# A fused attention and MLP kernel on one core: single-chunk blocks in the opening, w_in rounded at another place, two separating products in place of eight, and other places for the attention visits of groups 1 and 2

## The chip, the cores and the metric

The kernel runs on one core of a Trainium2 chip. The metric is device microseconds of one execution. The kernel before took 205.94 us (median of three runs, 205.86 to 206.51).

The engines carry short names: PE multiplies matrices (PEld is its weight load, which lies beside the multiplication), DVE is the vector engine, ACT the scalar engine with its activation tables, POOL the GpSimd engine, SP the engine that issues plain transfers. Each works through its own queue of instructions in order and waits on semaphores for the others.

## The reference

Linear attention with a decay for each head runs over 4 batches, 8 heads, 768 positions and 64 columns. Its output, put together over heads, is the input of an MLP with an exact GELU.

```
for b in range(nb):                                  # blocks of 64 positions
    intra = (qb @ kb.T * Dmask) @ vb                 # Dmask[i, j] = lam ** (i - j) for i >= j, else 0
    inter = (qb * lam_pow) @ kv_state                # lam_pow = lam ** (pos + 1)
    out   = intra + inter
    kv_state = lam ** block * kv_state + (kb * rev_pow).T @ vb     # rev_pow = lam ** (block - 1 - pos)
x = out.transpose(0, 2, 1, 3).reshape(3072, 512)
h = x @ w_in                                         # 512 x 2048
g = 0.5 * h * (1 + erf(h / sqrt(2)))
return g @ w_out                                     # 2048 x 512
```

## The kernel before

**Tiling.** The kernel takes blocks of 128 positions, which it calls chunks. There are 24: chunk n belongs to position block n // 4 and batch n % 4. Four chunks, one of each batch, make a group of 512 tokens; there are six groups. A chunk needs q, k and v (loaded by POOL with a conversion to bf16, line 68), k and q transposed (`kT`, `qT`), the scores k q in PSUM, masked by DVE into `sc_m` (line 201), and an output product from `sc_m` and the values (line 235). From its second position block on it also needs the product of q with the carried state (line 228). The output, emptied from PSUM into `x_t` (`empty_outputs`, lines 243 to 251), is the MLP's input, already transposed.

**MLP of a group.** The first product (`mm1`, line 421) takes 16 column tiles of `w_in`, called kf, each over four slices of the contraction, into a PSUM bank with the tag `mh`, and ACT applies the GELU (line 424) into `g_t`. A block of it can take several kf and only some of the tokens. In group 0 the second product is plain (`mm2`, line 434: 16 blocks, first those of chunks 0 and 1 in turn, then those of chunks 2 and 3). In groups 1 to 5 it is made of seven half-size products (`blocks_by_seven`, line 317) that run in the order m3, m4, m5, m2, m1, m6, m7, each for u = 0 and 1. Their left sides are sums of quarters of `g_t`, made on DVE (`g_sum`, line 291, each in two halves), and sums of the results on DVE follow (lines 355 to 401). The bank of m1 is read by DVE (line 387) before m7 adds to it again.

**PSUM.** A tag has two buffers in turn for `sc`, `mh` and `mo`, and one for `o` and `t`. A new tile in a buffer waits until the last reader of the old one is done.

**Order of the work.** The schedule is written by hand. Before the first MLP block the opening runs chunks 0 and 1 and the transposes of chunk 2, with idle products (`keep_warm`, line 484) between. In group 0 the dictionary `group0` (line 556) says which attention steps stand ahead of which block. For the rest, `at(when, run)` sorts steps by a place: g plus a share of the group's work, where B is one block of 2048 columns' worth. `visit(done, asked)` (line 588) puts attention products of two chunks at a time between blocks: for the chunks in `done` the state products in two turns and the output products, for those in `asked` the scores. Where there are chunks in `done` but none in `asked`, `apart_ps` (line 602) puts products of zeros between the two turns. `states_of` adds the products for the next state (line 209). `masks`, `empties`, `sums` and `new_states` are the DVE and ACT steps behind a visit.

**Loads.** POOL issues all loads of q, k, v, of `w_in` (but its first 256 columns) and of `w_out`, and between them scales the values (`v_dec`, line 155). The first 256 columns of `w_in` come by SP as float32 (`wide_w`, line 76) and ACT rounds them (line 512). From chunk 8 on, kT and qT are made by transposing transfers that SP issues (lines 176 and 177).

## Time and profile before

| | before |
|---|---|
| median of three runs | 205.94 us |
| the profiled execution, its own time | 206.0 us |
| span of the profiled execution | 204.2 us |
| PE busy | 197.0 us, 96% |
| DVE busy | 124.8 us, 61% |
| POOL busy | 96.2 us, 47% |
| ACT busy | 80.7 us, 39% |
| PE from its first idle product to its first MLP product | 1.19 to 14.29 us |
| group 0: first product, then second product | 14.29 to 32.27, 32.27 to 50.69 us |
| group 1: first product, then the seven products | 50.69 to 67.22, 67.22 to 82.81 us |
| group 2: first product | 82.81 to 100.25 us |

A stage is read as the PE's stretch from the first product of one kind to the first of the next; attention products lie within the stages. The start of an instruction is a point on one clock for all engines. The time of the execution is 1.8 us more than the span.

### The profile page before, as it was taken

The numbers are of one execution on the slowest core, as the hardware profiler recorded it, in microseconds if no ns is written. First come the engines' busy times: TensorE is split into PE (matmuls) and PEld (weight loads), VectorE is DVE, ScalarE is ACT, GpSimd is POOL, SyncE is SP. The second block draws the span as 40 slices with busy tenths as digits, with TensorE's granted clock in tenths as the row PEclk, the third lists the DMA queues.
The fourth block names the chain that finished last, engine by engine and source line by source line (L and its number), as shares of the span: only waits on it lengthen the run. The fifth ranks groups of instructions, "written<-read, shape, count | busy, mean of one in ns | idle before, by whom it ended". The sixth has DMA issues, their size and how long they took to land. (4 is left out here: it accounts for less than half of the span.)

```text
span 204.2 us, 4909 instructions
## 1 busy us (share of the span) xinstructions
PE 197.0 (96%) x2105; PEld 131.2 (64%) x2105; DVE 124.8 (61%) x202; ACT 80.7 (39%) x142; POOL 96.2 (47%) x112
## 2 busy tenths in 40 slices
PE   7889999999999999999999999999999999999992
PEld 2457574556874888646678646688645788445881
DVE  3743426773574699845999815968807857132482
ACT  4946653324565400273520273520264510477200
POOL 8999963899998922599998402000000000000000
PEclk9999999999999999999999999999999999999999
DMA  5999999999999999799999992200500000500014
GB/s 114 156 174 176 199 207 194 155 215 158 178 194 141 154 157 152 232 126 160 117 162 155 231 189 55 56 0 3 206 1 3 0 0 3 205 0 0 3 51 154
DMA packets 102373, 24.70 MB, mean 121 GB/s; under 512 B 92880, under 2 KB 99536, under 8 KB 102352
## 3 DMA queue, kind: packets, MB, share of 16 engines
q0 software_dynamic: 80688, 13.37, 89.4%
q1 hardware_dynamic: 21664, 11.02, 26.8%
q8 instruction: 16, 0.26, 0.5%
q14 instruction: 5, 0.04, 0.1%
HBM read 27.27 MB, written 6.29 MB: 164 GB/s over the span
## 5 line engine op out<-in xcount | busy, mean ns | idle before, releaser
L424 ACT ACTIVATE g_t<-h_ps 128x512 bf16<-128x512 f32 (+2 forms) x101 | 58.2, 576 | 82.0 <-PE h_ps L421 81.8
L421 PE MATMUL h_ps<-x_t,w_in_t 128*128 128x512 bf16 (+3 forms) x488 | 87.0, 334 | 0.4
L421 PEld LDWEIGHTS <-w_in_t 128*128 128x128 bf16 x488 | 44.1, 98 | 38.0 <-issue 1.3
L291 DVE TENSOR_TENSOR g_sum<-g_t 128x1024 bf16<-128x1024 bf16 x50 | 35.6, 752 | 12.6 <-ACT g_t L424 12.6
L317 PEld LDWEIGHTS <-g_sum 128*128 128x128 bf16 x400 | 38.6, 98 | 5.7 <-DVE g_sum L291 0.7
L155 POOL TENSOR_TENSOR v_dec<-v_t,lam_m 128x512 bf16<-128x512 bf16 x23 | 24.8, 1109 | 22.5 <-PE o_ps L235 10.2
L201 DVE TENSOR_TENSOR sc_m<-sc_ps,cmask 128x512 bf16<-128x512 f32 x40 | 25.4, 681 | 13.0 <-PE sc_ps L195 13.0
L68 POOL DMA_DIRECT2D k_t<-in_k_dram x24 | 22.3, 928 | 1.9 <-DMA w_out_t<-in_moe_w_out_dram 1.7
L68 POOL DMA_DIRECT2D v_t<-in_v_dram x24 | 21.7, 906 | 3.0 <-DMA w_out_t<-in_moe_w_out_dram 1.7
L68 POOL DMA_DIRECT2D q_t<-in_q_dram x24 | 21.8, 910 | 2.4 <-DMA w_out_t<-in_moe_w_out_dram 2.2
L317 PE MATMUL r_ps<-w_sum,g_sum 128*128 128x256 bf16 x160 | 19.1, 273 | 0.0
L317 PEld LDWEIGHTS <-g_t 128*128 128x128 bf16 x160 | 15.7, 98 | 2.9
L434 PE MATMUL o_ps<-w_out_t,g_t 128*128 128x512 bf16 x64 | 15.2, 379 | 0.0
L215 DVE TENSOR_TENSOR tmp<-kv_ps,state 128x512 f32<-128x512 f32 x8 | 5.1, 684 | 12.8 <-PE kv_ps L209 12.8
L251 DVE TENSOR_TENSOR x_t<-o_ps,lam_q 128x512 bf16<-128x512 f32 x16 | 10.5, 680 | 1.0 <-PE o_ps L235 1.0
L317 PE MATMUL p_ps<-w_out_t,g_sum 128*128 128x256 bf16 x80 | 9.7, 273 | 0.4 <-DVE g_sum L291 0.4
L434 PEld LDWEIGHTS <-g_t 128*128 128x128 bf16 x64 | 5.9, 98 | 6.2
L484 PE MATMUL idle_ps<-idle 128*128 128x256 bf16 (+1 forms) x33 | 8.6, 400 | 1.2 <-DVE idle L102 1.2
L317 PE MATMUL s_ps<-w_sum,g_sum 128*128 128x256 bf16 x80 | 9.6, 273 | 0.0
L317 PE MATMUL p_ps<-w_sum,g_t 128*128 128x256 bf16 x80 | 9.6, 273 | 0.0
L317 PE MATMUL q_ps<-w_sum,g_t 128*128 128x256 bf16 x80 | 9.6, 273 | 0.0
L317 PE MATMUL q_ps<-w_out_t,g_sum 128*128 128x256 bf16 x80 | 9.6, 273 | 0.0
(68 smaller groups left out, 153.4 us busy)
## 6 DMA issues: line engine op xcount, KB each, us to landing
out_dram<-o_sb SPq DMA_DIRECT2D x9, 512.0 KB, 2.8
k_t<-in_k_dram POOLq DMA_DIRECT2D x24, 128.0 KB, 6.9
q_t<-in_q_dram POOLq DMA_DIRECT2D x24, 128.0 KB, 7.4
v_t<-in_v_dram POOLq DMA_DIRECT2D x24, 128.0 KB, 7.3
w_out_t<-in_moe_w_out_dram POOLq DMA_DIRECT2D x4, 512.0 KB, 10.1
w_in_t<-in_moe_w_in_dram POOLq DMA_DIRECT2D x7, 256.0 KB, 7.3
out_dram<-o_sb SPq DMA_DIRECT2D x5, 256.0 KB, 6.0
wide_w<-in_moe_w_in_dram SPq DMA_DIRECT2D x1, 512.0 KB, 4.1
```

What stands on the lines that cost most here:

```text
L68: nc.gpsimd.dma_start(raw[n, name], chunk_of(name, n))
L155: eng.tensor_mul(c.v_dec, c.v, lam_m[:, :, None].to_broadcast((128, H, D)))
L201: nc.vector.tensor_mul(c.sc_m[:, :, hi, :], c.sc_ps[hi], mask)
L215: nc.vector.tensor_add(tmp, kv_ps, states[n])
L251: nc.vector.tensor_mul(c.x_o, c.o_ps, lam_q)
L291: nc.vector.tensor_tensor(gsum[i][:, ks, :], g_t[:, ka + k:ka + k + n4, ta], g_t[:, kb + k:kb + k + n4, tb], op=op)
L317: nc.tensor.matmul(o, left[i](k, slice(u * C, (u + 1) * C)), right[i](k), start=(begin and k == 0), stop=(k == KH - 1), skip_group_check=True)
L421: nc.tensor.matmul(h_ps[:, k, :], w_in_t[:, ki, (kf + k) * 128:(kf + k + 1) * 128], x_t[:, ki, cols], start=(k == 0 and ki == 0), stop=(ki ...
L424: nc.scalar.activation(g_t[:, kf:kf + ks, cols], h_ps, ACT.Gelu)
L434: nc.tensor.matmul(om[io], g_t[:, kf, io * C:(io + 1) * C], w_out_t[:, kf, :], start=(kf == 0), stop=(kf == NK2 - 1))
L484: nc.tensor.matmul(idle_ps[0][:, :cols], idle[:, :128], idle[:, :cols], start=True, stop=True)
```

## The change

- **Chunk 0's output** is emptied by DVE and no longer by ACT.
- **w_in** is rounded at the head of ACT's constants, before `make_powers`, and no longer behind chunk 0's output.
- **The opening** ends behind the scores of chunk 1. The outputs of chunk 1, the transposes of chunk 2 and idle products become steps of `group0`. The transposes of chunk 3 are split into k ahead of one block and q ahead of the next; k's use the bank `t`, and its scores follow at once.
- **Group 0's plan** for the first product has 19 blocks and no longer 21: four of two kf on one chunk (chunk 0 twice, chunk 1 twice), two of two kf on chunks 0 and 1, two of four kf on chunk 2, four of one kf on three chunks, three of four kf on chunk 3, four of one kf on all.
- **In the second product of group 0** the transposes of chunk 5 move two blocks later, the visit for the scores of chunks 4 and 5 two blocks, the transposes of chunk 6 two blocks, the visit that ends chunks 4 and 5 two blocks. `decay_v` of chunk 4 moves behind the transposes of chunk 4 in DVE's queue. The transposes of chunk 7 go to the head of group 1, the scores of chunks 6 and 7 to 2 B of group 1, their end to 6 B.
- **Group 1's plan** takes all its 16 blocks as two kf on half the tokens, first the eight of the lower half (chunks 4 and 5), then the eight of the upper. Its half sums of `g_t` start behind block 11. **Group 2's plan** takes its first eight blocks so.
- **Visits**: the scores of chunks 8 and 9 move from 13 to 15 B, the visit of 8 to 11 from 20 to 21 B (between the two halves of m5). The end of chunks 10 and 11 moves from 26 B of group 1 (ahead of m6) to 1 B of group 2, and takes the state products of chunks 8 to 11 with it, whose new states are made at 7 B and no longer 4 B. The scores of chunks 12 and 13 move from 1 B to 5 B of group 2.
- **Separating products**: two in each place and no longer eight. There are four places: the visits that end chunks 4 and 5, 6 and 7, 10 and 11, 22 and 23.

```diff
--- before.py
+++ after.py
@@ -243,7 +243,7 @@
     def empty_outputs(c):
         off = c.n % M
         c.x_o = xT[c.sb][:, :, off * C:(off + 1) * C]
-        if c.n == 2 * M - 1:
+        if c.n in (0, 2 * M - 1):
             nc.vector.tensor_copy(c.x_o, c.o_ps)
         elif c.n < 2 * M:
             nc.scalar.copy(c.x_o, c.o_ps)
@@ -296,13 +296,12 @@
         def with_sums(i, run):
             def both():
                 run()
-                if 10 <= i < 15:
-                    g_sum((5, 2, 1, 6, 7)[i - 10], 0)
+                if i in sums_at:
+                    g_sum((5, 2, 1, 6, 7)[sums_at.index(i)], 0)
             return both
 
-        done = [cost for _, cost in first]
-        blocks = [(with_sums((sum(done[:i]) + 4 * M * C - 1) // (4 * M * C), run), cost)
-                  for i, (run, cost) in enumerate(first)]
+        sums_at = range(11, 16) if g == 1 else range(10, 15)
+        blocks = [(with_sums(i, run), cost) for i, (run, cost) in enumerate(first)]
 
         left = {1: lambda k, t: gsum[1][:, k, t], 2: lambda k, t: gsum[2][:, k, t],
                 3: lambda k, t: g_t[:, k, t], 4: lambda k, t: g_t[:, KH + k, TH + t.start:TH + t.stop],
@@ -404,7 +403,7 @@
         blocks += [((lambda f=f, u=u: f(u)), KH * DH) for f in (m3, m4, m5, m2, m1, m6, m7) for u in range(2)]
         return blocks
 
-    N1 = 21
+    N1 = 19
 
     def mlp_blocks(g):
         T = M * C
@@ -443,14 +442,17 @@
         if g > 0:
             paired = [kf for k in range(NK2 // 2) for kf in (k, k + NK2 // 2)]
             plan = [(kf, 1, slice(0, T)) for kf in paired]
-            if g == 1:
-                plan = [(kf, 2, half) for half in (slice(0, T // 2), slice(T // 2, T)) for kf in (0, KH, 2, KH + 2)]
-                plan += [(kf, 1, slice(0, T)) for kf in paired[8:]]
+            if g < 3:
+                kfs = [kf for k in range(0, KH if g == 1 else KH // 2, 2) for kf in (k, k + KH)]
+                plan = [(kf, 2, half) for half in (slice(0, T // 2), slice(T // 2, T)) for kf in kfs]
+                plan += [(kf, 1, slice(0, T)) for kf in paired[len(plan):]]
             return blocks_by_seven(g, g_t, [(mm1(kf, n, cols), 4 * n * (cols.stop - cols.start))
                                             for kf, n, cols in plan])
-        two, three, third, fourth = slice(0, 2 * C), slice(0, 3 * C), slice(2 * C, 3 * C), slice(3 * C, T)
-        plan = [(kf, 1, two) for kf in range(6)] + [(0, 4, third), (4, 2, third)]
-        plan += [(kf, 1, three) for kf in range(6, 12)] + [(kf, 4, fourth) for kf in range(0, 12, 4)]
+        first, second, third, fourth = (slice(i * C, (i + 1) * C) for i in range(M))
+        two, three = slice(0, 2 * C), slice(0, 3 * C)
+        plan = [(kf, 2, chunk) for chunk in (first, second) for kf in (0, 2)] + [(4, 2, two), (6, 2, two)]
+        plan += [(0, 4, third), (4, 4, third)]
+        plan += [(kf, 1, three) for kf in range(8, 12)] + [(kf, 4, fourth) for kf in range(0, 12, 4)]
         plan += [(kf, 1, slice(0, T)) for kf in range(12, NK2)]
         assert len(plan) == N1
         blocks = [(mm1(kf, n, cols), 4 * n * (cols.stop - cols.start)) for kf, n, cols in plan]
@@ -492,6 +494,7 @@
     def causal(hi):
         nc.vector.tensor_mul(decay[:, hi], decay[:, hi], cmask[:, None, :].to_broadcast((128, HP, C)))
 
+    nc.scalar.copy(w_in_t[:, :, :256], wide_w)
     make_powers()
     nc.scalar.activation(warm, pos, ACT.Gelu)
     keep_warm(11, cols=512)
@@ -509,15 +512,9 @@
     keep_warm(3, new=False)
     transposed(c, "q", "mo", copy)
     outputs(live[0])
-    nc.scalar.copy(w_in_t[:, :, :256], wide_w)
     keep_warm(2)
     scores(c)
-    keep_warm(9, new=False)
-    outputs(live[1])
-    c = early(2)
-    transposed(c, "k", "mh", copy)
-    transposed(c, "q", "mo", copy)
-    keep_warm(1)
+    early(2)
     for n in range(3):
         decay_v(live[n], nc.gpsimd)
     for s in range(2):
@@ -548,27 +545,31 @@
         g, f = int(at), at - int(at)
         return round(f * total) if g == 0 else round(total + (g - 1 + f) * later)
 
-    def both_transposed(c):
-        transposed(c, "k", "mh", nc.vector.tensor_copy)
-        transposed(c, "q", "mo", nc.vector.tensor_copy)
+    def k_transposed(n):
+        transposed(live[n], "k", "t", copy)
+
+    def q_transposed(n):
+        transposed(live[n], "q", "mo", copy)
 
     e = N1
     group0 = {
-        1: [lambda: scores(live[2])],
+        0: [lambda: keep_warm(2, new=False)],
+        1: [lambda: keep_warm(7), lambda: outputs(live[1])],
+        2: [lambda: k_transposed(2)],
+        3: [lambda: q_transposed(2)],
+        4: [lambda: scores(live[2]), lambda: keep_warm(7)],
         5: [lambda: outputs(live[2])],
-        7: [lambda: next_states(0, next_products(0, "t"))],
-        8: [lambda: both_transposed(live[3])],
-        10: [lambda: scores(live[3])],
-        12: [lambda: outputs(live[3])],
-        17: [lambda: next_states(2, next_products(2, "t"))],
-        e: [w_out_sums, lambda: decay_v(live[4], nc.vector)],
+        7: [lambda: k_transposed(3)],
+        8: [lambda: q_transposed(3), lambda: next_states(0, next_products(0, "t")), lambda: scores(live[3])],
+        10: [lambda: outputs(live[3])],
+        18: [lambda: next_states(2, next_products(2, "t"))],
+        e: [w_out_sums],
         e + 8: [lambda: transposes(live[4])],
-        e + 9: [lambda: transposes(live[5], "o")],
-        e + 10: [lambda: visit([], [4, 5], "t o"), lambda: masks(5, 4)],
-        e + 11: [lambda: transposes(live[6])],
-        e + 13: [lambda: visit([4, 5], []), lambda: empties(4, 5)],
-        e + 14: [lambda: transposes(live[7])],
-        e + 15: [lambda: visit([], [6, 7], "t o"), lambda: masks(7, 6)],
+        e + 9: [lambda: decay_v(live[4], nc.vector)],
+        e + 11: [lambda: transposes(live[5], "o")],
+        e + 12: [lambda: visit([], [4, 5], "t o"), lambda: masks(5, 4)],
+        e + 13: [lambda: transposes(live[6])],
+        e + 15: [lambda: visit([4, 5], []), lambda: empties(4, 5)],
     }
 
     todo = []
@@ -597,10 +598,8 @@
             scores_by_quarters(live[n], tags)
         if done and not asked:
             apart = bank([128, HP, C], F32, "sc", "apart_ps")
-            for hp in range(HP):
-                for p in HALVES[::-1]:
-                    nc.tensor.matmul(apart[p, hp, :], idle[p, :D], idle[p, :C], start=True, stop=True,
-                                     skip_group_check=True)
+            for p in HALVES[::-1]:
+                nc.tensor.matmul(apart[p, 0, :], idle[p, :D], idle[p, :C], start=True, stop=True, skip_group_check=True)
         if done:
             from_states(done, o_ps, 1)
             for n, tag in zip(states_of, kv_tags.split()):
@@ -643,9 +642,9 @@
                 begin_at(g + w, n + i)
             at(g + 7 * B, lambda: prefetch(3 * M + 1))
             begin_at(g + 7 * B, n + 3)
-            visit_at(g + 13 * B, [], [n, n + 1], (masks, n + 1, n))
+            visit_at(g + 15 * B, [], [n, n + 1], (masks, n + 1, n), banks="t o")
             at(g + 11 * B, lambda: prefetch(4 * M - 1))
-            visit_at(g + 20 * B, [n, n + 1], [n + 2, n + 3], (masks, n + 3, n + 2), (empties, n, n + 1), banks="mh mh")
+            visit_at(g + 21 * B, [n, n + 1], [n + 2, n + 3], (masks, n + 3, n + 2), (empties, n, n + 1), banks="mh mh")
         else:
             states_of = (n, n + 2) if g < NG - 2 else ()
             visit_at(g + 10 * B, [n, n + 1], [n + 2, n + 3], (sums, *states_of), (masks, n + 3),
@@ -655,16 +654,18 @@
         for i, c_n in enumerate(later_on):
             begin_at(g + 0.57 + 0.03 * i, c_n)
         if g == 1:
-            visit_at(g + 26 * B, [n + 2, n + 3], [], (empties, n + 2, n + 3))
-            visit_at(g + 1 + 1 * B, [], later_on, (sums, n, n + 2), (masks, n + 5, n + 4),
-                     (g + 1 + 4 * B, new_states, n, n + 2), states_of=(n, n + 2), kv_tags="o t")
+            visit_at(g + 1 + 1 * B, [n + 2, n + 3], [], (empties, n + 2, n + 3), (sums, n, n + 2),
+                     (g + 1 + 7 * B, new_states, n, n + 2), states_of=(n, n + 2), kv_tags="mo mo")
+            visit_at(g + 1 + 5 * B, [], later_on, (masks, n + 5, n + 4))
         else:
             visit_at(g + 26 * B, [n + 2, n + 3], later_on, (empties, n + 2, n + 3))
             for w, (m, hi) in zip((26, 28, 31, 32), [(m, hi) for m in later_on for hi in range(2)]):
                 at(g + w * B, lambda m=m, hi=hi: masked(live[m], hi))
         for c_n in later_on:
             begin_at(g + 26 * B, c_n + 2)
-    visit_at(1 + 2 * B, [2 * M - 2, 2 * M - 1], [], (empties, 2 * M - 2, 2 * M - 1), (sums, M, M + 2),
+    at(1 + 0 * B, lambda: transposes(live[2 * M - 1]))
+    visit_at(1 + 2 * B, [], [2 * M - 2, 2 * M - 1], (masks, 2 * M - 1, 2 * M - 2))
+    visit_at(1 + 6 * B, [2 * M - 2, 2 * M - 1], [], (empties, 2 * M - 2, 2 * M - 1), (sums, M, M + 2),
              (new_states, M, M + 2), states_of=(M, M + 2), kv_tags="mo mo")
     todo.sort(key=lambda t: t[0])
 
```

## The prediction

> **What bounds the kernel.** I read the page's summary first, then the PE's rows in order of time, then for each gap the rows of the engine that ended it.
>
> ```profile
> span 204.2 us, 4909 instructions
> ...
> PE 197.0 (96%) x2105; PEld 131.2 (64%) x2105; DVE 124.8 (61%) x202; ACT 80.7 (39%) x142; POOL 96.2 (47%) x112
> ...
> PEclk9999999999999999999999999999999999999999
> ...
> PE 46%; DVE 2%; issue 0%
> ```
>
> PE is the bound, at full clock throughout, and the chain of work that ended last is PE's own from 104.75 us on. Column work is the same in both kernels and costs the same however it is cut: 40 products of 512 columns take 8.71 us on the chain (0.218 each), 16 of 256 take 1.75 (0.109), 16 of 128 start 0.89 apart (0.056 each). So the change can only win or lose in waits of PE, in the opening, and in the separating products. The table by stage shows where another engine is near:
>
> ```profile
> 14.29:32.27 17.98, 17.79 (x210) 12.08 (x208) 6.43 (x11) 10.79 (x22) 15.28 (x19) 1.00 1.50 195
> ...
> 67.22:82.81 15.59, 15.59 (x218) 13.36 (x217) 13.43 (x21) 1.77 (x3) 6.30 (x7) 1.00 1.86 144
> ```
>
> The columns are the stage, its length, the busy time of PE, PEld, DVE, ACT and POOL, the clock, the DMA share and GB/s. In the seven products of group 1 DVE is busy 13.43 of 15.59 us. Its queue there, and one of the same kind in group 2:
>
> ```profile
> 71.72 2.48 DVE L201 TENSOR_TENSOR sc_m<-sc_ps,cmask 128x512 bf16<-128x512 f32 x4 [2.10 <-PE sc_ps L195]
> ...
> 76.98 1.04 POOL L155 TENSOR_TENSOR v_dec<-v_t,lam_m 128x512 bf16<-128x512 bf16 x1 [4.24 <-DMA v_t<-in_v_dram]
> ...
> 77.11 1.45 DVE L291 TENSOR_TENSOR g_sum<-g_t 128x1024 bf16<-128x1024 bf16 x1
> ...
> 80.29 0.67 DVE L387 TENSOR_TENSOR f_x<-f_x,r_ps 128x512 f32<-128x512 f32 x1
> ...
> 81.01 1.91 PE L317 MATMUL r_ps<-w_sum,g_sum 128*128 128x256 bf16 x16
> ...
> 102.52 2.18 DVE L291 TENSOR_TENSOR g_sum<-g_t 128x1024 bf16<-128x1024 bf16 x1
> ...
> 103.08 1.06 POOL L155 TENSOR_TENSOR v_dec<-v_t,lam_m 128x512 bf16<-128x512 bf16 x1
> ...
> 104.75 1.49 PE L317 MATMUL p_ps<-w_out_t,g_sum 128*128 128x256 bf16 x12 [0.41 <-DVE g_sum L291]
> ```
>
> DVE runs without a pause from the masks at 71.72 to line 387, whose end (80.96) releases m7 at 81.01; PE could have had it at 80.84, so 0.17 us are lost. A `g_sum` that meets POOL's `v_dec` (0.68 alone) ends 0.54 us behind `v_dec`'s end in both pairs. The second costs PE 0.57 us in group 2 (four products of m5 end at 104.18, the fifth starts at 104.75).
>
> **The sum.** Base: the profiled execution, 206.0 us (span 204.2), 0.06 above the median 205.94.
>
> *Opening: -0.65.* The loads decide. POOL's and SP's queues keep their order, instruction for instruction. From start and time to landing: w1 (kf 2, 3) lands at 12.2, k2 13.1, q2 13.9, w2 (kf 4, 5) 10.12 + 6.0 = 16.1, w3 17.45, k3 18.3, q3 20.0, w4 21.5, w5 22.9. The rounding of w_in (1.05 us) moves ahead of the constants on ACT: table load and warm-up end at about 11.0 and no longer 9.93, hidden since the first GELU comes at 11.9. DVE empties chunk 0 at 10.5 to 11.2 (0.69, line 247), so the masks of chunk 1 end at 12.5 (12.38 before) and its outputs at 12.8. Then PE: block 0 at 11.25, block 1 at 12.8, block 2 at 13.6 (waits for ACT's copy of chunk 1, 0.59), block 3 at 14.25, the scores of chunk 2 at 14.9, seven idle products to 16.0, block 4 at 16.15 when w2 is there. By then 1.8 us of columns are done (four blocks of 0.45); before, 0.44 (14.29) + 0.96 (from 15.19) = 1.4. Left are 64 x 0.218 - 1.8 = 12.2 us of columns, 0.1 for the narrower cut, and small products from their rows: outputs 0.34 x 2 + 0.08, transposes 0.23 x 2, state products 0.46 x 2, scores 0.33, together 2.5. Waits: 0.3 for the scores of chunk 3 (q transposes to scores took 0.92, 13.94 to 14.86; 0.62 of it is covered by the k v products), 0.3 for its outputs (masks behind line 220 on DVE), 0.1 for banks. The second product starts at 16.15 + 15.5 = 31.6, not 32.27. The seven idle products ahead of block 4 lie in the wait for w2; were it there earlier, they would cost up to 0.76 (7 x 0.109). Bounds: -0.3 if w2 or w4 lands 0.3 later, -1.0 if my three waits are not there.
>
> *Separating products: -0.17 x 4 = -0.68.* Eight start 0.23 us before the next group (45.85, 46.08); two leave 0.06. Bound: 0, if the second turn waits for the first anyway.
>
> *Moves inside the second product of group 0: 0.* w_out's last quarter lands at about 35.7 and is needed at 36.7; k4, q4 land at 36.5 and 37.4 for 38.5, k5, q5 at 39.1 and 40.0 for 41.6, k6, q6 at 41.7 and 42.5 for 44.5, q7 at 46.9 for 48.7.
>
> *A new wait at the head of group 1: +0.87.* The transposes of chunk 7 now stand directly ahead of group 1's first block. Both use `mh`; block 0 takes the buffer of k's transpose, and so waits for ACT's copy of kT. That is queued behind the two copies of chunks 4 and 5 and behind `o_sb` of the last block.
>
> ```profile
> 46.39 0.64 PE L235 MATMUL o_ps<-sc_m,v_dec 128*64 128x128 bf16 x16
> ...
> 46.85 1.07 ACT L249 CAST x_t<-o_ps 128x512 bf16<-128x512 f32 x2 [2.50 <-PE o_ps L235]
> ...
> 48.26 0.59 ACT L164 COPY kT<-t_ps 128x512 bf16<-128x512 bf16 x1 [0.34 <-PE t_ps L161]
> ...
> 50.93 0.59 ACT L438 COPY o_sb<-o_ps 128x512 f32<-128x512 f32 x1 [0.95 <-PE o_ps L434]
> ```
>
> Counted from the visit's start V: output products 0.62 to 1.19, last block to 2.07, transposes to 2.51. ACT: copies 1.08 to 2.15, `o_sb` from 2.26 (its product ends at 2.23), kT from 2.74 (two copies start 0.48 apart, 1.07 - 0.59) to 3.33, block 0 at 3.38: 0.87 late. Before, a block of 0.88 and the scores lay between. Queued behind it is all of PE. Bounds 0 and 0.95.
>
> *Group 1, m7 uncovered: +1.49.* The visit at 21 B starts at 70.81 - 0.65 - 0.34 + 0.87 + 0.87 (m5's first half is now ahead of it) + 0.1 (one switch of tile shape) = 71.66. PE without waits reaches m7 1.58 + 0.87 + 3 x 1.746 = 7.69 later, at 79.35, because the visit of chunks 10 and 11 (1.36) no longer stands between m1 and m6. DVE's masks start 0.91 behind the visit, at 72.57, and line 387 has twelve instructions of 0.60 ahead of it: the half sum for m6 comes ninth, at 77.36, and meets the `v_dec` of 76.98 to 78.02, which waits for a load and so keeps its time. It ends at 78.56 as before, three more follow, line 387 starts at 80.29, m7 at 81.01: a wait of 1.66, against 0.17. Without `v_dec` m7 starts at 80.47, a wait of 1.12. I take the first: the sum lies whole within `v_dec`'s span.
>
> *Behind it: +0.1 and -0.57.* The visit of 10 and 11, its state products and the scores of 12 and 13 cost the same as before, but in one stretch more (0.1, as 52.44 to 52.52). PE then reaches the fifth product of m5 in group 2 at 105.48 (104.18 + 1.30, which is -0.65 - 0.51 + 0.87 + 1.49 + 0.1). DVE's half sum there starts 0.8 later than before, at 103.3, and ends between 103.9 (alone) and 105.4 (held by a `v_dec` of 103.74 to 104.8, POOL's chain starting 0.66 later from line 209): the old wait of 0.57 is gone. Bounds: -0.57 and +0.6.
>
> The sum: -0.65 - 0.68 + 0.87 + 1.49 + 0.1 - 0.57 = +0.56, to 206.6 of the profiled execution, **206.5 us** against the median.
>
> **A rule beside it.** By the Trainium skill, "SBUF — State Buffer", section "SBUF: two separate sides", a DVE operation with two inputs in SBUF and a GpSimd operation that reads SBUF exclude each other, and the one that starts first holds the ports for its whole instruction. The row at 77.11 agrees. The row at 102.52 does not: the sum starts 0.56 us before `v_dec` and still ends behind it. By the rule a sum that starts just ahead of `v_dec` loses nothing, which makes the slower rival below less likely.
>
> **The rivals.**
>
> *The line 387 chain misses `v_dec`* (206.0 us): m7 0.54 earlier, 206.5 - 0.5. For it: the meeting hangs on 0.4 us. Against it: before meets it with the same order. Chance 0.20.
>
> *The half sum of group 2 is held twice* (207.5, slower). Place: line 291 ahead of m5's fifth product. There POOL runs two `v_dec` (103.08 and 104.37 before, 0.66 later now). If the second follows the first without its gap, the two lie over the sum from 103.74 to 105.9, it ends at 106.4 and m5 waits 0.95 to 1.0. It decides from the point where that gap (0.23) closes. Against it: DVE took the sum between two `v_dec` at 104.1. Chance 0.20.
>
> *PE doesn't wait for the two PSUM buffers* (204.7, faster): both new waits are for a buffer's last reader, on ACT and on DVE; if the buffers are others or the readers done sooner than I count, 206.5 - 0.87 - 1.66 + 0.57 to 0.8 of the old wait in group 2 = 204.5 to 204.8 is left. For it: PE shows next to no waits now. Against it: both queues run in order, and DVE was late with more cover. Chance 0.18.
>
> **How the numbers follow.** About 0.3% (0.62 us, 205.3 to 206.6) is what can be told from no change. The forecast has 0.42, with its own range 206.0 to 207.0 by the opening's and the waits' bounds: 0.22 of it within 0.3%, 0.20 slower. The first rival gives 0.19 to the same and 0.01 to slower; the second 0.20 to slower; the third 0.18 to faster, of which 0.02 is the same. Faster 0.16, same 0.43, slower 0.41. The range 204.8 to 207.5 leaves 0.1 below (the third rival's lower half) and 0.1 above (the second's upper half).
>
> **What will show it.** Second product of group 0 at 31.6. ACT's copy of kT last before the first GELU of group 1, and a gap on PE of some 0.9 us between the transposes and line 420's first product. A gap of 1.1 to 1.7 us ahead of m7 in group 1, ended by line 386 on DVE. No gap in m5 of group 2. Four pairs of `apart_ps`. The forecast is wrong if one of the two gaps is under 0.4 us, or if the second product starts outside 31.2 to 32.0.

## The result, and the profile after

| | before | after |
|---|---|---|
| median (17 runs of each, on one chip) | 205.86 us (205.18 to 207.25) | 207.46 us (206.18 to 208.93) |
| ratio, 95% interval | | 1.0075 (1.005 to 1.010) |
| the profiled execution, its own time | 206.0 us | 206.91 us |
| second product of group 0 starts | 32.27 us | 31.75 us |
| group 1 starts | 50.69 | 50.24 |
| seven products of group 1 start | 67.22 | 67.37 |
| group 2 starts | 82.81 | 83.16 |
| seven products of group 2 start | 100.25 | 101.86 |
| group 3 starts | 114.74 | 115.77 |

The change makes the kernel slower, by 1.6 us of median. The two profiled executions differ by 0.9. In the experiments below a few executions fell into a slower state that any of these kernels can meet; medians, ranges and ratios there leave them out.

Two stages of the kernel before that were not shown yet, the second product of group 0 and the seven products of group 2 (stage and length, then the busy time of PE, PEld, DVE, ACT and POOL, clock, DMA share, GB/s):

```profile
32.27:50.69 18.42, 18.42 (x202) 9.94 (x201) 11.61 (x19) 5.68 (x10) 15.05 (x17) 1.00 2.16 179
...
100.25:114.74 14.49, 14.08 (x177) 12.20 (x176) 13.86 (x20) 1.77 (x3) 12.78 (x15) 1.00 2.06 151
```

The kernel after, in the same columns; its first stage starts at 11.41 and no longer at 14.29 because steps of the opening now lie within it:

```profile
11.41:31.75 20.34, 20.13 (x264) 14.96 (x262) 6.80 (x13) 11.08 (x21) 18.20 (x22) 1.00 1.62 190
31.75:50.24 18.49, 17.74 (x163) 9.42 (x162) 11.88 (x19) 6.16 (x11) 14.49 (x17) 1.00 2.13 180
...
67.37:83.16 15.79, 14.25 (x179) 12.19 (x177) 14.29 (x21) 1.77 (x3) 8.74 (x10) 1.00 2.06 154
...
101.86:115.77 13.91, 13.91 (x178) 12.28 (x177) 12.93 (x19) 1.77 (x3) 11.77 (x13) 1.00 2.10 154
```

PE now has holes in two stages that had none: 0.75 us (18.49 less 17.74) in the second product of group 0, and 1.54 us (15.79 less 14.25) in the seven products of group 1, where the kernel before was busy throughout. Group 2's seven products, the last of the four stages, lost their hole: PE is busy for 13.91 of 13.91 us, where it was busy for 14.08 of 14.49. The rows behind the holes, in the order of time:

```profile
49.12 0.59 ACT L437 COPY o_sb<-o_ps 128x512 f32<-128x512 f32 x1 [0.16 <-ACT x_t L249]
49.60 0.59 ACT L164 COPY kT<-t_ps 128x512 bf16<-128x512 bf16 x1
50.24 1.91 PE L420 MATMUL h_ps<-x_t,w_in_t 128*128 128x256 bf16 x16 [0.76 <-ACT kT L164]
...
77.38 1.04 POOL L155 TENSOR_TENSOR v_dec<-v_t,lam_m 128x512 bf16<-128x512 bf16 x1 [2.31 <-DMA v_t<-in_v_dram]
77.53 1.44 DVE L291 TENSOR_TENSOR g_sum<-g_t 128x1024 bf16<-128x1024 bf16 x1
79.02 1.48 PE L316 MATMUL s_ps<-w_sum,g_sum 128*128 128x256 bf16 x12 [0.64 <-DVE g_sum L291]
80.69 0.67 DVE L386 TENSOR_TENSOR f_x<-f_x,r_ps 128x512 f32<-128x512 f32 x1
81.41 1.91 PE L316 MATMUL r_ps<-w_sum,g_sum 128*128 128x256 bf16 x16 [0.91 <-DVE f_x L386]
...
105.35 1.91 PE L316 MATMUL p_ps<-w_out_t,g_sum 128*128 128x256 bf16 x16
```

- At 50.24 group 1's first block starts behind ACT's copy of kT, which stands behind `o_sb`. The last four transposing products start at 49.10 and PE takes 0.22 us for them; it could have started the block at about 49.34, so 0.9 us are lost.
- From 77.53 a half sum meets POOL's `v_dec` and takes 1.44 us. It ends 0.55 us behind `v_dec`'s end. m6's fifth product waits for it (0.64), and m7 for line 386, which stands behind three more instructions in DVE's queue (0.91). m6 and m7 together come 1.87 us later than without waits: m6 starts at 77.79, m7 would at 79.53, and it starts at 81.41.
- At 105.35 the 16 products of m5 in group 2 run in one piece; before, the fifth of them came 0.57 us late.

### The profile page after: what moved, and what is told of

The parts are those of the page before. It is cut to its first block, busy times and chain, and to the rows that moved or that the text cites. A ratio compares the mean times of both kernels' runs of the same rounds, so it can differ in the third digit from the quotient of the medians.

```text
span 205.1 us, 5045 instructions
## 1 busy us (share of the span) xinstructions
PE 196.8 (96%) x2175; PEld 138.1 (67%) x2175; DVE 125.2 (61%) x203; ACT 79.7 (39%) x139; POOL 96.5 (47%) x112
## 4 chain that ended last, share of the span: by engine, by line
PE 87%; DVE 5%; DMA 2%; POOL 2%; issue 1%; ACT 0%; POOLq 0%
PE h_ps L420 41%; PE p_ps L316 8%; PE r_ps L316 8%; PE q_ps L316 8%; PE o_ps L433 7%; PE s_ps L316 4%; PE sc_ps L195 3%; PE o_ps L235 3%; PE o_ps L228 2%; DMA q_t<-in_q_dram 2%; PE t_ps L161 1%; PE kv_ps L209 1%; PE idle_ps L486 1%; DVE sc_m L201 1%; POOL k_t L68 1%
## 5 line engine op out<-in xcount | busy, mean ns | idle before, releaser
L420 PEld LDWEIGHTS <-w_in_t 128*128 128x128 bf16 x576 | 51.0, 98 | 32.2 <-issue 1.6
L486 PE MATMUL idle_ps<-idle 128*128 128x256 bf16 (+1 forms) x39 | 9.6, 385 | 1.2 <-DVE idle L102 1.2
```

The costliest lines, as they stand in the source:

```text
L420: nc.tensor.matmul(h_ps[:, k, :], w_in_t[:, ki, (kf + k) * 128:(kf + k + 1) * 128], x_t[:, ki, cols], start=(k == 0 and ki == 0), stop=(ki ...
L486: nc.tensor.matmul(idle_ps[0][:, :cols], idle[:, :128], idle[:, :cols], start=True, stop=True)
```

## The experiments

Each stands beside the kernel before on the same chip (205.47 to 205.96 us in the sets of runs), and the ratio with its 95% interval is to that kernel; it need not be the quotient of two medians. The changed kernel's ratio is 1.0075 (1.005 to 1.010). Stages come from the one profiled execution that each kernel has.

### The wait at the head of group 1

**Another bank for k's transpose.**

```diff
-    at(1 + 0 * B, lambda: transposes(live[2 * M - 1]))
+    at(1 + 0 * B, lambda: transposes(live[2 * M - 1], "o"))
```

> The transposes of chunk 7's k go to the bank o, so that group 1's first block no longer waits for ACT's copy of kT; the order of every engine is that of the changed kernel. Theory (the gap at the head of group 1, 0.90 us, is a wait for a PSUM buffer and its price goes straight to the end): the gap falls under 0.15 us and the time by 0.8 to 0.9, to a ratio of about 1.003; if the half sum for m6 then runs ahead of the v_dec that held it (77.38 in the changed kernel), up to 0.8 more. Rival (m7 in group 1 is held at a fixed point by POOL's v_dec, which waits for a load): the gap closes, but m7 starts at 81.0 to 81.4 as before and nothing is gained, ratio 1.007.

Measured: 207.66 us, ratio 1.0096 (1.0061 to 1.0132). From the second product of group 0 to the seven products of group 1 it takes 35.54 us, in the changed kernel 35.62. The profile of this kernel, ACT's and PE's rows:

```profile
51.16 0.60 ACT L423 ACTIVATE g_t<-h_ps 128x512 bf16<-128x512 f32 x1 [0.20 <-PE h_ps L420]
51.81 1.03 PE L420 MATMUL h_ps<-x_t,w_in_t 128*128 128x256 bf16 x8 [0.68 <-ACT g_t L423]
...
73.49 0.61 PE L316 MATMUL p_ps<-w_out_t,g_sum 128*128 128x256 bf16 x4 [1.33 <-DVE g_sum L291]
```

The first block starts at once, but the second waits until the first one's GELU ends (51.76), so it is in that block's buffer. The wait moved by one block and nothing was gained: the loss stays, as the rival said, but not by the rival's mechanism. The third line is another thing: in this execution four half sums took 4.94 us, with two `v_dec` over them, and m5 of group 1 waited 1.33.

**kT emptied by DVE.**

```diff
+    def transposes_7():
+        transposed(live[2 * M - 1], "k", "mh", nc.vector.tensor_copy)
+        transposed(live[2 * M - 1], "q", "mh", scaled)
+
-    at(1 + 0 * B, lambda: transposes(live[2 * M - 1]))
+    at(1 + 0 * B, transposes_7)
```

> The changed kernel, with the transposed k of chunk 7 emptied by DVE and no longer by ACT. Theory (the wait at the head of group 1 is ACT's queue: two copies, o_sb, kT, then the first GELU; changing the bank only handed the wait on): the gap of 0.90 us closes and no other opens behind it, first block's GELU ends before block 2 asks for its bank; second product of group 0 to the seven products of group 1 goes from 35.62 us to 34.75, time -0.8 against the changed kernel, ratio to before 1.003. Rival: the wait passes to the next bank again, as with the other bank, 35.5 and no gain, ratio 1.0075.

Measured: 206.54 us, ratio 1.004 (1.0013 to 1.0068). Rows of DVE and PE:

```profile
50.13 0.42 DVE L164 COPY kT<-t_ps 128x512 bf16<-128x512 bf16 x1 [2.50 <-PE t_ps L161]
...
50.62 1.92 PE L420 MATMUL h_ps<-x_t,w_in_t 128*128 128x256 bf16 x16 [0.37 <-DVE kT L164]
```

No queue stands ahead of the copy, but the copy itself lies between the transposes and the block: 0.37 us of the wait stay, and the two stages (second product of group 0, first product of group 1) take 35.23 us and not 34.75. No wait opens behind it in group 1's first product. So 0.4 of the 0.9 us were ACT's queue; the expectation held in direction and had the size too large. In the time the gain is not clear: the ratio's interval overlaps with that of the changed kernel.

### The waits of m6 and m7 in group 1

**The end of chunks 10 and 11 back ahead of m6.**

```diff
-            visit_at(g + 1 + 1 * B, [n + 2, n + 3], [], (empties, n + 2, n + 3), (sums, n, n + 2),
+            visit_at(g + 26 * B, [n + 2, n + 3], [], (empties, n + 2, n + 3))
+            visit_at(g + 1 + 1 * B, [], [], (sums, n, n + 2),
                      (g + 1 + 7 * B, new_states, n, n + 2), states_of=(n, n + 2), kv_tags="mo mo")
```

> The end of chunks 10 and 11 goes back to 26 B of group 1, between m1 and m6; their state products stay at 1 B of group 2, all else as in the changed kernel. Theory (m7 waits for DVE's line 386, and the visit was the cover): PE's waits ahead of m6's fifth product and of m7 (0.64 + 0.91 us, m7 1.87 later than unhindered) shrink to 0.4 to 0.6 in all, m7 still starts at about 81.4, and the 1.3 us of the visit are gone from group 2; of it 0.3 to 0.6 come back as the old wait in m5 of group 2. Gain 0.7 to 1.3, ratio 1.001 to 1.004. Rival (the visit is only moved, PE's work is the same, and DVE is later still by the two copies of chunks 10 and 11): gain under 0.3, ratio 1.006 to 1.0075.

Measured: 206.56 us, ratio 1.0032 (1.0004 to 1.0061). The PE's rows of m6 and m7:

```profile
79.46 1.92 PE L316 MATMUL s_ps<-w_sum,g_sum 128*128 128x256 bf16 x16
81.36 1.91 PE L316 MATMUL r_ps<-w_sum,g_sum 128*128 128x256 bf16 x16
```

Both waits are gone but for 0.15 us of m7. From the seven products of group 1 to group 3 it takes 47.32 us, in the changed kernel 48.40; 0.4% of the time comes back by the two ratios, about 0.9 us, though the two intervals still touch. Of the old wait in m5 of group 2, 0.22 us came back. PE's work is the same in both, only its place differs: in its old place the visit (1.2 us of PE) covers DVE's queue. But the place is not all that differs in this execution. The half sum for m6 escaped the delay too, since it starts 0.08 us ahead of `v_dec`:

```profile
78.23 0.68 DVE L291 TENSOR_TENSOR g_sum<-g_t 128x1024 bf16<-128x1024 bf16 x1
...
78.31 1.50 POOL L155 TENSOR_TENSOR v_dec<-v_t,lam_m 128x512 bf16<-128x512 bf16 x1 [3.81 <-DMA v_t<-in_v_dram]
```

Here it is `v_dec` that takes longer, 1.50 us for 1.04. What the place and the meeting are worth by themselves is read below from four profiles.

**`v_dec` of chunk 14 on DVE, behind the seven products.**

```diff
+    def begin_14():
...
-            begin_at(g + 26 * B, c_n + 2)
+            if c_n + 2 == 14:
+                at(g + 26 * B, lambda: begin_14())
+                at(g + 1 + 0.5 * B, lambda: nc.vector.tensor_mul(
+                    live[14].v_dec, live[14].v, lam_m[:, :, None].to_broadcast((128, H, D))))
+            else:
+                begin_at(g + 26 * B, c_n + 2)
```

> The scaled values of chunk 14 are made by DVE at the head of group 2, where it is idle, and not by POOL at 77.4; all else as in the changed kernel. Theory (a half sum of g_t cannot run while POOL's v_dec runs): the half sum for m6 takes 0.68 and not 1.44 us, m7 in group 1 starts 0.7 to 0.8 earlier, and 0.4 to 0.8 of it reach the end, ratio 1.004 to 1.0055. Rival (the long half sum has another cause, such as POOL's issues of loads): the half sum stays at 1.4 us or another one takes the delay, ratio 1.007.

Measured: 206.9 us, ratio 1.0059 (1.0022 to 1.0095), and 15.49 us for the seven products of group 1 in place of 15.79. Rows of DVE and PE:

```profile
69.69 4.17 DVE L291 TENSOR_TENSOR g_sum<-g_t 128x1024 bf16<-128x1024 bf16 x4
...
79.31 1.48 PE L316 MATMUL s_ps<-w_sum,g_sum 128*128 128x256 bf16 x12 [0.33 <-DVE g_sum L291]
81.70 1.91 PE L316 MATMUL r_ps<-w_sum,g_sum 128*128 128x256 bf16 x16 [0.91 <-DVE f_x L386]
```

The sum for m6 takes 0.68 us without `v_dec` beside it, but m7 gains only 0.3: it starts 1.58 us late in place of 1.87. The four sums ahead of the masks took 4.17 us here (3.35 in the changed kernel) because another `v_dec` lay over the last of them, and so DVE's masks started 1.38 us behind the visit and not 0.91. Without these 0.47 m7 would be 1.11 us late. So the meeting with `v_dec` is the smaller part of that wait; DVE's unbroken queue up to line 386 is the rest. In the time the gain is not clear: the intervals overlap.

**Bank and old place together**, the first and the third edit in one kernel:

```diff
-    at(1 + 0 * B, lambda: transposes(live[2 * M - 1]))
+    at(1 + 0 * B, lambda: transposes(live[2 * M - 1], "o"))
...
-            visit_at(g + 1 + 1 * B, [n + 2, n + 3], [], (empties, n + 2, n + 3), (sums, n, n + 2),
+            visit_at(g + 26 * B, [n + 2, n + 3], [], (empties, n + 2, n + 3))
+            visit_at(g + 1 + 1 * B, [], [], (sums, n, n + 2),
```

> The other bank for chunk 7 and the end of chunks 10 and 11 back at 26 B of group 1. Theory (the two waits are independent and their prices add): 1.5 to 2.2 us under the changed kernel, 205.3 to 206.0, ratio 0.997 to 1.000, and the opening's 0.5 and the separating products' 0.7 become visible. Rival (DVE's queue or the loads set group 1's end): the two together gain no more than the better of them alone, ratio 1.001 to 1.004.

Measured: 205.84 us, ratio 1.0028 (1.000 to 1.0056), the rival's figure: no more than the old place alone (1.0032). The waits of m6 and m7 are gone again, and the second block waits for the GELU (51.44, 0.68 us), as with the bank alone. Its profile shows in the opening what the next experiments are about:

```profile
16.80 1.05 PE L420 MATMUL h_ps<-x_t,w_in_t 128*128 128x256 bf16 x8 [0.62 <-DMA w_in_t<-in_moe_w_in_dram]
```

**What the place and the meeting are worth.** In four profiles DVE's masks start the same 0.91 us behind PE's visit, so m7 can be compared in them: how late it starts, counted from the start of m6 and 1.746 us of products.

| | half sum for m6 held by `v_dec` | not held |
|---|---|---|
| end of chunks 10 and 11 behind m7 | 1.87 us (the changed kernel) | 1.12 us (other bank) |
| ahead of m6, the old place | 0.68 us (the version with three mends, below) | 0.01 us (bank and old place) |

The meeting with `v_dec` costs 0.7 to 0.8 us in either row, and the missing cover 1.1 to 1.2 in either column, which is the length of the visit that was moved. Whether the meeting comes about differs from execution to execution.

### What the gains ahead of group 2 are worth

**The kernel before with the new opening, and nothing else.** The edit is the parts of the change in the opening, in group 0's plan and in `group0` up to the second product; its core:

```diff
-        plan = [(kf, 1, two) for kf in range(6)] + [(0, 4, third), (4, 2, third)]
-        plan += [(kf, 1, three) for kf in range(6, 12)] + [(kf, 4, fourth) for kf in range(0, 12, 4)]
+        plan = [(kf, 2, chunk) for chunk in (first, second) for kf in (0, 2)] + [(4, 2, two), (6, 2, two)]
+        plan += [(0, 4, third), (4, 4, third)]
+        plan += [(kf, 1, three) for kf in range(8, 12)] + [(kf, 4, fourth) for kf in range(0, 12, 4)]
...
+    nc.scalar.copy(w_in_t[:, :, :256], wide_w)
     make_powers()
```

> Kernel before with the new opening and the new plan of group 0's first product, nothing else of the change. In six profiles with this opening the second product started at 31.5 to 31.75 us plus the wait that a load of w_in left (0.6 to 0.9 us in four of them). Theory: the term of -0.65 is true where w2 and w3 land early and lost where not; with the second product at 31.6 to 32.5, the time within 0.3 us of before, ratio 0.999 to 1.001, with more spread. Rival (the prediction's term holds on average): 205.0 where before is 205.65, ratio 0.997.

Measured: 206.05 us, ratio 1.0005 (0.9976 to 1.0034). In this profile no load of w_in was late:

```profile
16.37 1.05 PE L421 MATMUL h_ps<-x_t,w_in_t 128*128 128x256 bf16 x8
...
31.74 1.46 PE L434 MATMUL o_ps<-w_out_t,g_t 128*128 128x512 bf16 x6
...
64.49 0.42 PE L195 MATMUL sc_ps<-qT,kT 64*64 64x128 bf16 x16 [0.56 <-DMA qT<-q_t]
```

The second product starts 0.53 us earlier than in the kernel before, and group 1 too (50.15). Then the scores of chunk 9 wait 0.56 us for the transposing transfer of its q, and the seven products of group 1 start at 67.44, in the kernel before at 67.22. In this execution the gain is given back whole.

**The kernel before with two separating products**, the change's edit in `visit` alone.

```diff
-            for hp in range(HP):
-                for p in HALVES[::-1]:
-                    nc.tensor.matmul(apart[p, hp, :], idle[p, :D], idle[p, :C], start=True, stop=True,
-                                     skip_group_check=True)
+            for p in HALVES[::-1]:
+                nc.tensor.matmul(apart[p, 0, :], idle[p, :D], idle[p, :C], start=True, stop=True, skip_group_check=True)
```

> Kernel before, with two separating products in place of eight and nothing else. Theory: each of three places gives 0.17 us (turn end to next group 0.23 -> 0.06); at the fourth (end of chunks 10, 11 in group 1) PE is 0.17 us ahead of m7 anyway, which DVE's line 387 releases, so nothing is gained there: 0.5 us, ratio 0.9975, the distance from the first turn's end to the second turn 0.23 before and 0.06 here. Rival: the second turn waits for the first whatever stands between, ratio 1.000.

Measured: 205.77 us, ratio 1.0022 (0.9996 to 1.0047): a gain of 0.25% lies outside the interval, and a loss is not clear either. The places gave what was counted (18.25 us from the second product of group 0 to group 1, before 18.42; 83.59 from group 3 to the last m7, before 83.76), but:

```profile
71.80 0.42 PE L195 MATMUL sc_ps<-qT,kT 64*64 64x128 bf16 x16 [0.57 <-DMA qT<-q_t]
```

PE came to the scores of chunk 11 0.2 us earlier than in the kernel before, and waited 0.57 us for the transfer of its q. That transfer landed at 71.67 here and at 69.19 in the kernel before, so the loss is this execution's, and how often it comes is not shown.

**Less work early in the kernel before.**

```diff
-                for kf in range(part * 4, part * 4 + 4):
+                for kf in range(part * 4, part * 4 + 4) if (io > 1 or part != 1) else ():
```

> Kernel before without eight of the 512-column products in group 0's second product (kf 4 to 7 for chunks 0 and 1, left out of the output): 8 x 0.218 = 1.74 us less of PE at about 33 to 36 us. Theory (from there to some 72 us PE stands just behind the loads: with 0.33 us gained ahead of it, the scores of chunk 11 waited 0.57 us for the transposing transfer of its q): PE arrives 1.74 us earlier, the landing does not move, waits of 1 to 1.7 us for DMA open between 38 and 72 us, and the time falls by 0.2 to 0.7 us only, ratio 0.9965 to 0.999. Rival (PE alone sets the pace, that wait was chance): the time falls by 1.7, ratio 0.9917, no wait for DMA over 0.4 us.

Measured: 206.98 us, ratio 1.0018 (0.9989 to 1.0048). PE's rows with a wait in the second product of group 0, and the first of group 1:

```profile
39.40 0.40 PE L161 MATMUL t_ps<-ident,k_t 128*128 128x128 bf16 x4 [0.45 <-DMA k_t<-in_k_dram]
40.23 0.40 PE L161 MATMUL t_ps<-ident,q_t 128*128 128x128 bf16 x4 [0.43 <-DMA q_t<-in_q_dram]
...
43.52 0.40 PE L161 MATMUL t_ps<-ident,q_t 128*128 128x128 bf16 x4 [0.27 <-DMA q_t<-in_q_dram]
...
50.66 0.60 PE L421 MATMUL h_ps<-x_t,w_in_t 128*128 128x256 bf16 x4
```

1.74 us of PE's work are gone, and group 1 starts at 50.66 where it started at 50.69. The three waits for loads took the saving. At the first of these rows PE is 1.09 us ahead of the kernel before (which is there at 40.49), at the second 0.48 (40.71), at the third 0.04 (43.56). In the kernel before the same loads were early: q of chunk 5 landed at 39.96, 0.75 us ahead of its use, and q of chunk 6 at 42.51, 1.05 us ahead; here q of chunk 6 landed at 43.48. So a saving in this place is kept only as far as the loads are ahead, and that changes by up to a microsecond between executions. The expected waits opened, 1.15 us in all; the expected gain of 0.2 to 0.7 us did not show.

**The changed kernel with the old opening**, and **the same with kT on DVE and the end of chunks 10 and 11 in its old place**. The first puts the diff above back, line for line:

```diff
-    N1 = 19
+    N1 = 21
...
-    nc.scalar.copy(w_in_t[:, :, :256], wide_w)
     make_powers()
```

The second adds the edits of kT on DVE and of the old place:

```diff
-    at(1 + 0 * B, lambda: transposes(live[2 * M - 1]))
+    at(1 + 0 * B, transposes_7)
...
-            visit_at(g + 1 + 1 * B, [n + 2, n + 3], [], (empties, n + 2, n + 3), (sums, n, n + 2),
+            visit_at(g + 26 * B, [n + 2, n + 3], [], (empties, n + 2, n + 3))
+            visit_at(g + 1 + 1 * B, [], [], (sums, n, n + 2),
```

> The changed kernel, with the opening and the first product of group 0 as in the kernel before (21 blocks, w_in rounded behind chunk 0's output); all from the second product of group 0 on stays changed. Theory: the new opening gains only what the loads of w_in leave over: the second product started at 31.75, 32.52, 32.14, 32.34, 32.15 us in five profiles with it (mean 32.2) and at 32.27 in the old one, so this is within 0.25 us of the changed kernel, ratio to before 1.006 to 1.0085, with the second product at 32.1 to 32.4 and a narrower spread. Rival (the prediction's term): the new opening is worth 0.5 to 0.65 us, so this is slower than the changed kernel, ratio 1.010 to 1.011.

> The changed kernel with three things altered: old opening and first product of group 0, transposed k of chunk 7 emptied by DVE, and the end of chunks 10 and 11 back ahead of m6 in group 1. What is left of the change: two separating products, the plans and visits of groups 1 and 2, the places in the second product of group 0. Theory: against the changed kernel -0.87 (head of group 1), -1.1 (m6 and m7, from the profiles), opening 0: 205.5 where that is 207.4, ratio to before 0.998 (the separating products' 0.5 kept). Rival (the moved visits cost PE something by themselves, such as the narrower products): 206.2 or more, ratio above 1.002.

Measured: 207.95 us, ratio 1.011 (1.0072 to 1.0147), and 207.01 us (205.69 to 207.67), ratio 1.0067 (1.0041 to 1.0093). Both fell out against the theory and at the figures of the rivals. The second product starts at 32.24 us in both, but the profiles wait for the transfer of chunk 11's q, 0.66 us in the first and 1.67 in the second:

```profile
74.23 0.42 PE L195 MATMUL sc_ps<-qT,kT 64*64 64x128 bf16 x16 [1.67 <-DMA qT<-q_t]
```

In the first, m5 of group 2 also waits 0.73 us for a half sum (108.00). The second kernel with the new opening, in the next section, is 0.9% better, so with the rest of the change the old opening came out worse than the new one, though beside the rest of the kernel before they are equal; for the first kernel the intervals overlap. It is not an earlier second product that makes this difference (32.24 here, 33.28 in the profile of the better one). Why those transfers come later wasn't settled; one profile of each is not enough for a landing that moves by more than a microsecond from one execution to the next.

### A version with both waits mended

**The changed kernel with kT on DVE and the end of chunks 10 and 11 back**, new opening kept, and **the same with k's transpose in `o` too**. To the last diff, on the changed kernel, the second adds:

```diff
-        transposed(live[2 * M - 1], "k", "mh", nc.vector.tensor_copy)
+        transposed(live[2 * M - 1], "k", "o", nc.vector.tensor_copy)
```

> The changed kernel, new opening kept, with the end of chunks 10 and 11 back ahead of m6 in group 1 (alone it gave 0.9 us of median) and the transposed k of chunk 7 emptied by DVE (alone 0.9). Theory (the two waits are apart and their gains add, but what is ahead of the loads is given back): 205.6, ratio 0.998 to 1.001. Rival (they add in full, and nothing is given back): 205.0 or less, ratio 0.9965 or below, a version that beats both kernels.

> The changed kernel with the end of chunks 10 and 11 back ahead of m6 in group 1, the transposed k of chunk 7 emptied by DVE, and its bank changed to o, so that the first block of group 1 waits neither for ACT nor for DVE. Theory: the 0.36 us that PE still waited there with DVE's copy alone close too, second product of group 0 to seven products of group 1 34.8 us (35.24 with DVE's copy alone, 34.95 in the kernel before), time 205.1 to 205.4 where the kernel before takes 205.7 to 205.95, ratio 0.996 to 0.998, and better than both kernels. Rival (what PE gains ahead of the loads is given back): the stage shorter, the time as with DVE's copy alone or a wait for a transfer behind it, ratio 0.998 to 1.000.

Measured: 205.36 us (204.88 to 207.12), ratio 0.9974 (0.9948 to 1.0001), and 206.13 us (205.57 to 207.10), ratio 1.0032 (1.0011 to 1.0052). The first lies between its theory (0.998) and its rival (0.9965); it is 1% or 2 us better than the changed kernel, and its best run is 0.3 us under the best of the kernel before in that set (205.19); that it beats that one is likely, not certain. The second missed both its theory and its rival. The bank brings back the wait that it made in the first experiment, though DVE empties kT, and in this profile the half sum for m6 was held by `v_dec` again. ACT's, PE's and DVE's rows:

```profile
50.95 0.60 ACT L423 ACTIVATE g_t<-h_ps 128x512 bf16<-128x512 f32 x1 [0.69 <-PE h_ps L420]
...
51.60 1.03 PE L420 MATMUL h_ps<-x_t,w_in_t 128*128 128x256 bf16 x8 [0.69 <-ACT g_t L423]
...
78.01 1.52 DVE L291 TENSOR_TENSOR g_sum<-g_t 128x1024 bf16<-128x1024 bf16 x1
```

The second block starts 0.05 us behind the end of the first one's GELU. I had counted on buffers that alternate with each new tile; with one tile less in `mh`, two blocks in a row seem to use the same one. That is read from the wait; the addresses were not looked at.

## Why the prediction was right in its waits and too low in its sum

The forecast was 206.5 us, 0.3% slower, at the edge of what can be told from no change; 207.46 was measured, 0.8% slower. That lies outside the forecast's own range (206.0 to 207.0) and only 0.04 us inside the whole one, whose upper end stood there for a rival that the profile does not show. That it lies inside is luck.

- **New wait at the head of group 1, +0.87:** 0.9 in the profile, ended by ACT's copy of kT, as said.
- **m7 uncovered, +1.49:** m7 starts 1.87 us late (1.66 counted), in two pieces, 0.64 ahead of m6's fifth product and 0.91 ahead of m7. `v_dec` did not keep its time: it came at 77.38, 0.40 us later than counted. For the case that the sum is not held the prediction counted 1.12, and the profile with the other bank shows 1.12. The rule of the Trainium skill, "SBUF — State Buffer", section "SBUF: two separate sides", that the operation which starts first holds the ports, agrees with the row here: the sum starts 0.15 us behind `v_dec` and ends behind it. It also agrees with the row at 78.23 in the experiment with the old place, where the sum starts first and `v_dec` is the one that takes longer. The row at 102.52 of the kernel before, which the prediction held against the rule, is another case: POOL was not idle there but issued a load (from 102.19, 0.88 us), and `v_dec` followed at once. Whether such an issue holds the sum was not tested.
- **Old wait of m5 in group 2, -0.57:** gone, as said. Of the ten profiles with this part of the change, three others have about 0.2 us of it and one has 0.73 (the changed kernel with the old opening).
- **Separating products, -0.17 each:** the places that can be read alone show it. Two of the four stand ahead of group 1's seven products; that the gain lasts there isn't shown (below).
- **Moves in the second product of group 0, 0:** no wait there in the profile of the kernel after.
- **The rivals.** In this profile the chain didn't miss `v_dec` (in that with the other bank it did); the half sum of group 2 wasn't held; PE did wait for both buffers.
- **The opening, -0.65, is the step that failed.** In the one profile it was 0.52 (31.75). Over nine profiles of kernels with the new opening the second product starts at 31.74 to 33.28, mean 32.31 us; over five with the old one at 32.24 to 32.39, mean 32.30. In all nine it starts 14.03 or 14.04 us behind the first product of kf 6 and 7, so this block decides. The new plan has it at 17.7 us, the old one at 20.8. In seven of the nine it starts 0.04 to 0.07 us behind the landing of its load, which came at 17.66 to 18.45; I had counted with 17.45, and my bound named the loads of w2 and w4 but not this one, w3. In the other two the first product itself started late (11.95 and 13.09, elsewhere 11.09 to 11.50), behind chunk 0's q.

In five of the nine profiles a block waits 0.55 to 0.87 us for w_in; the longest such row, from the experiment with the other bank:

```profile
18.49 1.94 PE L420 MATMUL h_ps<-x_t,w_in_t 128*128 128x256 bf16 x24 [0.87 <-DMA w_in_t<-in_moe_w_in_dram]
```

The mistake behind it is that I took a shorter PE stage for a shorter kernel, without asking how far ahead of their use the loads land. With 1.74 us less work nothing was left of the saving at the head of group 1. Of the small gains, one execution each lost 0.56 us at chunk 9's q (new opening alone) and 0.57 at chunk 11's (two separating products); neither kernel came out faster than the one before.

Stage by stage the rest of the sum fits the profile of the changed kernel. From the second product of group 0 to group 1's seven products it takes 0.67 us more than before (+0.87 - 0.34 = 0.53 counted), from there to group 3 0.88 more (+1.49 + 0.1 - 0.57 - 0.17 = 0.85 counted), and from group 3 to the last m7 0.17 less, as counted. Without the -0.65 the sum is +1.21 us; 1.6 were measured, with an interval of 1.0 to 2.1. What makes the rest is not shown: the medians of the kernel before alone differ by 0.5 us between sets of runs, and the profiled execution of the changed kernel, with an early second product and 206.91 us, is one of its better ones. One finding stands against this reading: with the other waits mended, the kernel with the new opening was 0.9% faster than that with the old one, though its second product started no earlier.

## What to carry to other kernels

Before a gain on the busiest engine is counted, follow it to the next place where that engine needs something that lands by itself: if the landing has less slack than the gain, the gain ends there, and leaving out work of the same size is a cheap way to measure it. A step that stands between a slow queue and its reader has a price when it is moved, even if the busiest engine's work stays the same: list what its time covered, instruction by instruction, on the other engine's queue. And when a buffer is changed to remove a wait, ask who takes the freed turn, since the wait may only move to the next tile.

## What the runs showed of the hardware that was not expected

- A half sum took 1.54 us (0.68 alone) in the changed kernel, among the three sums from 69.60 us that took 2.75 together, with nothing but load issues on POOL between 67.7 and 73.0 us. Single sums of 1.52 and 1.53 us with only load issues beside them stand in two other profiles (70.29 with `v_dec` of chunk 14 on DVE, 71.95 with two mends), while other sums beside such issues took 0.68. So an overlap with `v_dec` is not the only thing that slows such a sum; what did it here is open.
- The transposing transfers of q hold their queue for 1.2 us but take about 7.5 us from issue to landing while the loads run (median of the six from 50 to 75 us in the changed kernel), and that of chunk 11's q landed at 71.7, 73.6 and 74.2 us in the three profiles that waited for it. A schedule that reads them with little slack differs from execution to execution.
